# Unread matmuls of constants in TensorE's head: a gated linear attention recurrence followed by a squared-ReLU MLP

## The chip, the cores and the metric

The kernel runs on one core of a Trainium2 chip. The metric is the device time of one execution in microseconds (us), as the median of several runs. Before the change three runs took 197.0, 198.0 and 198.47 us, so the median is 198.0 us. One further execution was taken with the hardware profiler: it took 196.32 us, of which its profile covers a span of 194.6 us.

## The reference

For each of 4 batches and 8 heads a 48 x 48 state is decayed row by row, gets an outer product added, and is read by a query, for 768 steps. The 8 x 48 = 384 outputs of each of the 3072 tokens then go through a two-layer MLP of width 2048 with a squared ReLU.

```python
def _attn_ref(q, k, v, alpha):
    for t in range(S):                       # S = 768, D = 48
        state = alpha[:, :, t, :, None] * state + np.einsum('bhd,bhe->bhde', k[:, :, t], v[:, :, t])
        y[:, :, t] = np.einsum('bhd,bhde->bhe', q[:, :, t], state)
    return y

def _moe_ref(x, w_in, w_out):                # x: (3072, 384), w_in: (384, 2048), w_out: (2048, 384)
    h = x @ w_in
    r = np.maximum(h, 0.0)
    g = r * r
    return g @ w_out
```

## The kernel before, in words

**Tiling.** The tokens are cut into 24 chunks of 128 (6 for each batch). Within a chunk the recurrence is done as matrix products. For chunk g, in the order of its steps:

- Four loads on SP's queue (L384): alpha, k, q and v into one of 8 raw buffers, 192 KB each.
- `decay`: ACT takes the logarithm of alpha (`lab`, L394); TensorE makes running sums over the chunk with the triangular constant `LTRI` (L400, L402, into `psG`); ACT takes three exponentials (`asb` L406 and L408, `acs` L411); DVE scales k and q (`qks`, L417); GpSimd casts v (`vbf`, L421).
- `turned`: TensorE transposes the scaled k and q against the constant `IDENT` (8 matmuls, L432), and DVE copies them out (`qkt`, L435).
- `scores`: TensorE, 8 matmuls (L447); DVE masks the two results (`pm`, L453).
- `carry`: TensorE makes the chunk's contribution to the state (L467), DVE adds it (`ust`, L474), GpSimd decays it into the next state (`sbf`, L484).
- `mixed`: TensorE, state and scores times their right sides (L496, L500); ACT copies out (`xbf`, L507).
- `placed`: TensorE transposes the chunk's result (3 matmuls, L517), ACT writes it to `xt` (L521).
- `up`: four units for each chunk, each of 12 matmuls of 128 columns (L537) into one of two buffers `psH`; ACT applies the ReLU (`rr`, L542), DVE squares (`gt`, L544). Unit u of any chunk reads quarter u of the first weight matrix, `win`.
- `down`: four parts for each chunk, each of 4 matmuls of 384 columns (L553), accumulated in one of two buffers `psO`; after the fourth, ACT copies out (`osb`, L559) and SP stores (L561). Part p reads quarter p of the second weight matrix, `wout`.

**Order.** Nothing is ordered by hand. Every step is entered with its engine, an estimated duration and a due time (`add`); `order()` simulates the engines and the two load queues and fixes one order of instructions for each engine; `plan()` then places the waits on semaphores between engines. On the chip each engine runs its own list strictly in that order: an instruction that waits holds back everything behind it on its engine.

**The loads of the head.** The weights come in quarters on GpSimd's queue, tied to SP's loads: `weights` gates the first quarter of each group on the landing of a chunk's alpha, and `loads` gates the alpha load of chunks 3, 4 and 5 on the landing of a weight quarter. So the head contains this chain: GpSimd casts v of chunk 1, issues `win` quarters 0 and 1 (L365); when quarter 0 lands, SP issues alpha of chunk 3; when that lands, GpSimd issues `win` 2 and 3 and `wout` 0 and 1 (L369); when `wout` 0 lands, SP issues alpha of chunk 4; when that lands, GpSimd issues `wout` 2 and 3; when `wout` 2 lands, SP issues alpha of chunk 5. SP issues its loads in order.

**TensorE's order in the head**, the same in both kernels as far as the real work goes: sums 0, transposes 0, sums 1, scores 0, carry 0, transposes 1, mixed 0, placed 0, scores 1, sums 2, carry 1, mixed 1, transposes 2, placed 1, up unit 0 of chunk 0, scores 2, carry 2, up unit 1 of chunk 0, mixed 2, sums 3, placed 2, transposes 3, carry 3, scores 3, up unit 2 of chunk 0, mixed 3, then five up units without a break (the first of chunk 1, the last of chunk 0 and three more of chunk 1), and then the first down part. The kernel's two constants are written by GpSimd at the start (L338 to L343).

Of the kernel before, what the change touches and what calls it, by code (L numbers as in the profile page):

```python
# [32 lines left out]
class Program:  # L33
# [18 lines left out]
    def add(self, eng, fn, work, at, reads=(), writes=(), dma=None, nbytes=0, fast=False, behind=None):  # L52
        op = Op(len(self.ops), eng, fn, work, at, dma, nbytes, fast)
        for r in reads:
            for w in self.writer.get(r, ()):
                op.deps[w.n] = "raw"
        for r in writes:
            for w in self.writer.get(r, ()):
                op.deps.setdefault(w.n, "waw")
            for w in self.readers.get(r, ()):  # L60
                op.deps.setdefault(w.n, "war")
        for r in reads:
            if r not in writes:
                self.readers.setdefault(r, []).append(op)
        for r in writes:
            self.writer[r] = [op]
            self.readers[r] = []
        if dma is not None:
            last = self.slots.get(dma)
            if last is not None:  # L70
                op.deps.setdefault(last.n, "war")
            self.slots[dma] = op
        op.deps.pop(op.n, None)
        if behind is not None:
            op.deps.setdefault(behind.n, "order")
        self.ops.append(op)
        return op

    def order(self):
# [16 lines left out]
        def done(op, t, users):  # L96
            for u in users:
                known[u.n] = max(known[u.n], t)
                missing[u.n] -= 1
                if not missing[u.n]:  # L100
                    release(u, known[u.n])
# [42 lines left out]
        while left:  # L144
            best = None
            for e in ENGINES:
# [5 lines left out]
                while w and w[0][0] <= free[e]:  # L152
                    _, at, n = heapq.heappop(w)
# [13 lines left out]
            while w and w[0][0] <= t:  # L167
                _, at, n = heapq.heappop(w)
                heapq.heappush(r, (at, n))
            _, n = heapq.heappop(r)  # L170
            op = self.ops[n]
# [10 lines left out]
            else:  # L182
                same = [u for u in op.users if u.eng == e]
                done(op, free[e], same)
                done(op, free[e] + self.LATENCY[e], [u for u in op.users if u.eng != e])
        self.programs = programs

    def plan(self):
        place = {}
# [65 lines left out]
def bass_gla_recurrent__then__act_relu_squared_kernel(  # L255
# [21 lines left out]
    FT = DFF // 128  # L277
# [9 lines left out]
    NXB, NGT, NRR, NOS, NU, NAC = 2, 5, 4, 4, 2, 3  # L287

    def sb(name, shape, dt, n=None):
        if n is None:  # L290
            return nc.alloc_sbuf_tensor(name, shape, dt)
        return [nc.alloc_sbuf_tensor(f"{name}{i}", shape, dt) for i in range(n)]
# [13 lines left out]
    LTRI = sb("ltri", [128, 128], BF16)  # L306
    IDENT = sb("ident", [128, 128], BF16)
# [7 lines left out]
    psO = [nc.alloc_psum_tensor(f"psO{i}", [128, 512], FP32) for i in range(2)]  # L315
    psG = [nc.alloc_psum_tensor(f"psG{i}", [128, 512], FP32) for i in range(4)]

    pr = Program(nc)
    add = pr.add
# [33 lines left out]
    WH = 4  # L353
# [174 lines left out]
    def up(b, u, at):  # L528
# [4 lines left out]
        def mm(pe):  # L533
# [10 lines left out]
        add("DVE", lambda dve: dve.tensor_tensor(GT[b % NGT][:, FU * u:FU * u + FU, :], RR[r][:], RR[r][:], ALU.mult),  # L544
            430, at, reads=[("rr", r)], writes=[("gt", b % NGT, f) for f in range(FU * u, FU * u + FU)])

    def down(b, tt, p, at):
        n = CPB * b + tt
        ps, key, o = psO[n % 2], ("psO", n % 2), n % NOS

        def mm(pe):
            for fj in range(4 * p, 4 * p + 4):
                last = pe.matmul(ps[:, 0:DM], GT[b % NGT][:, fj, tt * 128:(tt + 1) * 128], WOUT[:, fj, :],  # L553
                                 start=(fj == 0), stop=(fj == FT - 1))
            return last
        add("PE", mm, 650, at, reads=[("gt", b % NGT, f) for f in range(4 * p, 4 * p + 4)] + [("wout", 4 * p * WH // FT)],
            writes=[key])
        if p == 3:
            add("ACT", lambda act: act.activation(OSB[o][:], ps[:, 0:DM], AF.Copy), 490, at,  # L559
                reads=[key], writes=[key, ("osb", o)])  # L560
            add("SP", lambda sp: sp.dma_start(out[n * C:(n + 1) * C, :], OSB[o][:]), 600, at,  # L561
                reads=[("osb", o)], dma=f"osb{o}", nbytes=C * DM * 4, fast=True)
# [8 lines left out]
    for b in range(NB):  # L571
        base = CPB * b + CPB + LAG
        for u in range(NU_):
            stages.append((base + u * CPB / NU_, lambda at, b=b, u=u: up(b, u, at)))
        for i in range(4 * CPB):
            stages.append((base + CPB + CPB / NU_ / 2 + i * CPB / (4 * CPB),
                           lambda at, b=b, i=i: down(b, i // 4, i % 4, at)))
    for at, fn in sorted(stages, key=lambda s: s[0]):
        fn(at)

    pr.order()
    pr.plan()

    with nc.Block() as block:
# [49 lines left out]
```

## Time and profile before

| what | value |
|---|---|
| median of three runs (lowest, highest) | 198.0 us (197.0, 198.47) |
| the profiled execution, and its span | 196.32 us, 194.6 us |
| TensorE matmuls busy in the span | 179.1 us (92%), 2464 instructions |
| ACT, DVE, GpSimd busy | 125.9 us, 118.7 us, 39.2 us |
| share of the chain that ended last on TensorE | 83% |
| the same for transfers (DMA) | 10% |
| TensorE busy from 50 to 160 us | 109.99 of 110 us |
| up matmuls (L537) | 1152, 222 ns each in the mean, 81.1 us |
| down matmuls (L553) | 384, 326 ns each in the mean, 76.6 us |
| weight quarters `win`, issue to landing | 5.5 to 7.0 us |
| weight quarters `wout`, issue to landing | 6.2 to 9.2 us |

How to read it. A busy time of a matmul runs from its start to its modelled end, and matmuls overlap, so the start of the next instruction says more of the pace than the duration of one. "Granted clock" is TensorE's clock as a share of full speed, recorded by the profiler. The chain that ended last is followed back from the last instruction, at each step to what released it. Durations and starts below are from that one execution, in us from the start of its span.

### The profile page before, as it was taken

Reading aid. Unit: us, or ns where it says so; the run is one execution under the profiler, and the core shown is the slowest. Engines: PE = TensorE matmul, PEld = TensorE weight load, DVE = VectorE, ACT = ScalarE, POOL = GpSimd, SP = SyncE. Lnnn points to the kernel's source line nnn. Section 1 sums busy time; section 2 is a strip of 40 time slices with the busy share of each in tenths; the row PEclk is TensorE's granted clock in tenths of the full one; section 3 lists DMA queues with packets and bytes.
Section 4 is the critical chain, followed back from the end, with each engine's and each line's share of the span. In section 5 each row is a group of like instructions: output and inputs, shape, how many; then the busy total and the mean of one; then the engine's idle time right before and its main releaser. Section 6 shows DMA issues by size and latency. Waiting matters only on the chain.

```text
span 194.6 us, 5761 instructions
## 1 busy us (share of the span) xinstructions
PE 179.1 (92%) x2464; PEld 143.5 (74%) x2464; DVE 118.7 (61%) x223; ACT 125.9 (65%) x261; POOL 39.2 (20%) x72
## 2 busy tenths in 40 slices
PE   1568589999999999999999999999999999999994
PEld 0346378787788878878877887888878887887772
DVE  4475754483657775775776775676677577585230
ACT  3534626747777766875786786786686687565751
POOL 2162541421111133133100302312110320220000
PEclk9999859999999999999999999999999999999999
DMA  6999899999989999898989979991110110111012
GB/s 124 204 188 163 159 173 203 142 167 189 207 174 190 187 187 228 180 221 166 226 190 214 221 158 211 193 215 70 45 40 3 40 44 0 44 44 40 3 40 81
DMA packets 107033, 27.11 MB, mean 139 GB/s; under 512 B 100352, under 2 KB 107008, under 8 KB 107008
## 3 DMA queue, kind: packets, MB, share of 16 engines
q1 hardware_dynamic: 103296, 23.60, 56.5%
q0 software_dynamic: 3712, 3.15, 11.3%
q8 instruction: 19, 0.31, 0.7%
q14 instruction: 6, 0.05, 0.1%
HBM read 25.17 MB, written 4.72 MB: 154 GB/s over the span
## 4 chain that ended last, share of the span: by engine, by line
PE 83%; DMA 10%; SPq 3%; ACT 1%; issue 1%; POOL 0%
PE psH L537 33%; PE psO L553 32%; DMA win<-in_moe_w_in_dram 6%; PE psG L432 5%; PE psG L447 3%; SPq L384 3%; PE psG L400 3%; DMA raw<-in_v_dram 2%; DMA raw<-in_alpha_dram 2%; PE psG L500 2%; PE psG L517 2%; PE psG L496 2%; PE psG L467 1%; PE psG L402 1%; ACT rr L542 1%
## 5 line engine op out<-in xcount | busy, mean ns | idle before, releaser
L537 PE MATMUL psH<-xt,win 128*128 128x128 bf16 x1152 | 81.1, 222 | 0.4
L542 ACT ACTIVATE rr<-psH 128x512 bf16<-128x512 f32 x96 | 57.1, 597 | 35.5 <-PE psH L537 34.8
L553 PE MATMUL psO<-wout,gt 128*128 128x384 bf16 x384 | 76.6, 326 | 0.0
L537 PEld LDWEIGHTS psH<-xt,win 128*128 128x128 bf16 x1152 | 69.1, 99 | 3.0 <-ACT rr L542 1.1
L544 DVE TENSOR_TENSOR gt<-rr 128x512 bf16<-128x512 bf16 x96 | 40.8, 426 | 39.9 <-ACT rr L542 39.9
L453 DVE TENSOR_TENSOR pm<-psG,ltri 128x512 bf16<-128x512 f32 x48 | 32.7, 688 | 17.7 <-PE psG L447 17.7
L553 PEld LDWEIGHTS psO<-wout,gt 128*128 128x128 bf16 x384 | 33.1, 97 | 13.8
L421 POOL CAST vbf<-raw 128x384 bf16<-128x384 f32 x24 | 14.1, 589 | 97.3 <-PE psG L500 49.4
L417 DVE TENSOR_TENSOR qks<-raw,asb 128x768 bf16<-128x768 f32 x24 | 22.8, 951 | 6.5 <-ACT asb L408 6.4
L484 POOL TENSOR_TENSOR sbf<-ust,acs 64x192 bf16<-64x192 f32 x32 | 17.5, 548 | 28.4 <-DVE ust L474 25.8
L435 DVE COPY qkt<-psG 128x1024 bf16<-128x1024 bf16 x24 | 16.6, 692 | 5.4 <-PE psG L432 4.8
L432 PE MATMUL psG<-ident,qks 128*128 128x128 bf16 x192 | 16.3, 234 | 3.7 <-DVE qks L417 3.7
L432 PEld LDWEIGHTS psG<-ident,qks 128*128 128x128 bf16 x192 | 13.6, 105 | 6.6 <-DVE qks L417 4.3
L394 ACT ACTIVATE lab<-raw 128x384 bf16<-128x384 f32 x24 | 12.5, 520 | 8.0 <-DMA raw<-in_alpha_dram 8.0
L521 ACT ACTIVATE xt<-psG 128x384 bf16<-128x384 bf16 x24 | 11.8, 491 | 6.6 <-PE psG L517 6.5
L559 ACT ACTIVATE osb<-psO 128x384 f32<-128x384 f32 x24 | 11.7, 488 | 6.2 <-PE psO L553 2.8
L406 ACT ACTIVATE asb<-psG 128x384 bf16<-128x384 f32 x24 | 11.8, 490 | 4.6 <-PE psG L402 3.4
L507 ACT ACTIVATE xbf<-psG 128x384 bf16<-128x384 f32 x24 | 11.8, 490 | 3.2 <-PE psG L500 3.1
L400 PE MATMUL psG<-lab,ltri 128*128 128x384 bf16 x24 | 8.5, 356 | 4.3 <-ACT lab L394 4.3
L408 ACT ACTIVATE asb<-psG 128x384 bf16<-128x384 f32 x24 | 11.8, 491 | 0.8
L500 PE MATMUL psG<-vbf,pm 128*128 128x48 bf16 x192 | 12.0, 189 | 0.0
L500 PEld LDWEIGHTS psG<-vbf,pm 128*128 128x128 bf16 x192 | 10.4, 100 | 1.5 <-DVE pm L453 0.3
(28 smaller groups left out, 102.6 us busy)
## 6 DMA issues: line engine op xcount, KB each, us to landing
raw<-in_alpha_dram SPq DMA_DIRECT2D x24, 192.0 KB, 3.9
raw<-in_k_dram SPq DMA_DIRECT2D x24, 192.0 KB, 4.1
raw<-in_q_dram SPq DMA_DIRECT2D x24, 192.0 KB, 4.2
raw<-in_v_dram SPq DMA_DIRECT2D x24, 192.0 KB, 3.8
out_dram<-osb SPq DMA_DIRECT2D x24, 192.0 KB, 3.1
win<-in_moe_w_in_dram POOLq DMA_DIRECT2D x4, 384.0 KB, 6.2
wout<-in_moe_w_out_dram POOLq DMA_DIRECT2D x4, 384.0 KB, 7.7
```

Of the source, the lines that this page charges most:

```text
L400: pe.matmul(ps[:, 0:HD], LTRI[:], LAB[l][:, :, 0:D])
L417: return dve.tensor_tensor(QKS[x][:, :, :, 0:D], in0, in1, ALU.mult)
L421: add("POOL", lambda e: e.tensor_copy(VBF[vb][:], RAW[r][:, 2, :]), 550, at, reads=[("raw", r, 2)], writes=[("vbf", vb)])
L432: last = pe.matmul(pt[:, j, :], flat[:, j * 128:(j + 1) * 128], IDENT[:], is_transpose=True)
L435: add("DVE", lambda dve: dve.tensor_copy(QKT[t][:].rearrange("p h s -> p (h s)"), ps[:].bitcast(BF16)), 700, at, reads=[key], writes=[key, ...
L453: add("DVE", lambda dve, i=i, ps=ps: dve.tensor_tensor(PMB[m][:, i, :, :], ps[:].rearrange("p (j s) -> p j s", j=NP), mask, ALU.mult), 690 ...
L484: add("POOL", lambda e, p0=p0, e0=e0, ac=ac: e.tensor_tensor(SBF[new][p0:p0 + 64, :, e0:e0 + D], UST[u][p0:p0 + 64, :, e0:e0 + D], ac, ALU ...
L500: last = pe.matmul(ps[:, h * D:(h + 1) * D], PMB[m][:, i, j, :], VBF[vb][:, h * D:(h + 1) * D], start=first, stop=(first or i == 1))
L537: last = pe.matmul(ps[:, f, :], WIN[:, kt, fj * 128:(fj + 1) * 128], XT[:, kt, b * TB:(b + 1) * TB], start=(kt == 0), stop=(kt == KT - 1))
L542: add("ACT", lambda act: act.activation(RR[r][:], ps[:], AF.Relu), 600, at, reads=[key], writes=[key, ("rr", r)])
L544: add("DVE", lambda dve: dve.tensor_tensor(GT[b % NGT][:, FU * u:FU * u + FU, :], RR[r][:], RR[r][:], ALU.mult), 430, at, reads=[("rr", r) ...
L553: last = pe.matmul(ps[:, 0:DM], GT[b % NGT][:, fj, tt * 128:(tt + 1) * 128], WOUT[:, fj, :], start=(fj == 0), stop=(fj == FT - 1))
```

## The change

`fill` is a new method of the planner. After `order()` has fixed the order, it goes through TensorE's list up to the first down part. Wherever the planner's own timetable leaves TensorE idle before an operation, it inserts as many matmuls as fit into 0.75 of that gap at 217 ns each. The inserted matmuls multiply `IDENT` by `LTRI` repeated four times (512 columns) into the two `psO` buffers. Nothing reads the result: the first matmul of a down part overwrites it. Besides these, one group of six such matmuls is entered as a step with an early due time; it waits for GpSimd's two constants.

The built kernel has 47 inserted matmuls, in 13 groups: 7 before sums 0, 7 before transposes 0, 2 before sums 1, 6 before transposes 1, 2 before placed 0, 4 before mixed 1, 2 before transposes 2, 2 before up unit 0, 4 before up unit 1, 6 before placed 2, 2 before carry 3, 2 before up unit 2, and 1 after mixed 3. The order of all other instructions on the five engines, and their waits, are as before, but for TensorE's wait for GpSimd's constants, which has moved from sums 0 and transposes 0 to the first inserted matmul.

```diff
+    def fill(self, fn, each, share, until):
+        out = []
+        end = None
+        for op in self.programs["PE"]:
+            if op is until:
+                until = None
+            if until is not None and end is not None and (op.start - end) * share > each:
+                n = int((op.start - end) * share / each)
+                idle = Op(len(self.ops), "PE", lambda pe, n=n: fn(pe, n), n * each, 0.0)
+                idle.start = end
+                self.ops.append(idle)
+                out.append(idle)
+            out.append(op)
+            end = op.start + op.work
+        self.programs["PE"] = out
...
+    downs = []
+
+    def busy(pe, n):
+        for i in range(n):
+            last = pe.matmul(psO[i % 2][:], IDENT[:], bass.AP(tensor=LTRI, offset=0, ap=[[128, 128], [0, 4], [1, 128]]))
+        return last
+
+    add("PE", lambda pe: busy(pe, 6), 2000, -6, reads=["ident", "ltri"], writes=[("psO", 0), ("psO", 1)])
+
...
-        add("PE", mm, 650, at, reads=[("gt", b % NGT, f) for f in range(4 * p, 4 * p + 4)] + [("wout", 4 * p * WH // FT)],
-            writes=[key])
+        op = add("PE", mm, 650, at, reads=[("gt", b % NGT, f) for f in range(4 * p, 4 * p + 4)] + [("wout", 4 * p * WH // FT)],
+                 writes=[key])
+        downs.append(op)
...
     pr.order()
+    first = next(o for o in pr.programs["PE"] if o in downs)
+    pr.fill(busy, 217, 0.75, first)
     pr.plan()
```

## The prediction

> **What bounds the kernel now.** I read the granted clock by stretches first, then the chain of waits, then the order of instructions around each load. From 50 us on TensorE is busy without a gap, and its last matmuls (20 of L553, start 188.27) end with the kernel but for one copy and a store. So the change can only move the moment from which TensorE no longer waits. The question is which moment that is.
>
> The clock, in windows of the head. Columns: window, its length, busy time of the five engines (instructions), granted clock, DMA share, GB/s.
>
> ```profile
> 22.50:23.00 0.50, 0.00 (x0) 0.00 (x0) 0.13 (x1) 0.47 (x2) 0.50 (x1) 1.00 0.69 138
> 23.00:23.50 0.50, 0.00 (x0) 0.00 (x0) 0.10 (x1) 0.47 (x3) 0.50 (x2) 0.80 0.91 108
> 23.50:24.00 0.50, 0.00 (x0) 0.00 (x0) 0.50 (x1) 0.46 (x2) 0.50 (x2) 0.50 0.71 104
> ...
> 30.00:30.50 0.50, 0.50 (x11) 0.50 (x9) 0.00 (x0) 0.04 (x1) 0.00 (x0) 0.87 1.31 200
> ```
>
> Between full and half speed, 0.80 puts the fall at 23.3 and 0.87 the rise at 30.13. The clock column also says 1.00 in every earlier window, but there the durations must be read: 12 up matmuls take 1.49 us at 17.78 and 0.83 us at 19.97. TensorE therefore ran at half speed up to about 19.9, fast to 23.3, at half speed to 30.13. The three turns lie 3.4 and 6.8 us apart, once and twice the same step.
>
> The chain of waits through the head. Columns: start, duration, what.
>
> ```profile
> 11.58 5.64 DMA win<-in_moe_w_in_dram
> ...
> 17.24 3.90 DMA raw<-in_alpha_dram
> ...
> 21.43 5.49 DMA win<-in_moe_w_in_dram
> ...
> 26.96 1.48 PE psH L537 x12
> ...
> 28.46 0.61 ACT rr L542
> ...
> 29.11 1.98 PE psH L537 x24
> ...
> 31.11 1.51 PE psH L537 x24
> ```
>
> Up to 26.92 loads set the time: each weight quarter opens an alpha load and that opens the next quarters. Only behind that does TensorE's half speed lie on the path, for some 3 us. But the load chain runs on beside it, which the order of instructions shows:
>
> ```profile
> 41.22 0.37 SPq L384 DMA_DIRECT2D raw<-in_alpha_dram  x1
> ...
> 44.24 1.46 PE L553 MATMUL psO<-wout,gt 128*128 128x384 bf16 x8
> ...
> 44.88 0.52 ACT L394 ACTIVATE lab<-raw 128x384 bf16<-128x384 f32 x1 [0.21 <-DMA raw<-in_alpha_dram]
> ...
> 45.54 0.33 PE L400 MATMUL psG<-lab,ltri 128*128 128x384 bf16 x1
> ```
>
> The alpha load of chunk 5 is issued at 41.22 when `wout` 2 lands, ACT sits idle 0.21 us for it, the logarithm ends at 45.40, and the sums of chunk 5 start at 45.54. No engine's speed is in that chain.
>
> **The change part by part.**
>
> *One inserted matmul.* No row has 512 columns. By the pace of starts, 12 up matmuls take 1.27 us at half speed (26.96 to 28.23), 106 ns for 128 columns, and 0.67 us fast; four 384-column down matmuls take 0.65 us fast, 163 ns each. By columns I estimate 423 ns at half speed and 217 ns fast; the bounds are 163 ns (the 384-column row) and 423. Their weight load (98 ns fast, 151 ns slow for L537) runs beside them. 47 of them are 10.2 us fast, 19.9 us slow.
>
> *Before 17.2 us (30 of the 47: 7, 7, 2, 6, 2, 4, 2).* The constants are ready at 2.08 (L343). The first seven at half speed end at about 5.1, so sums 0 start 0.8 us late (4.27 before). TensorE is then busy without a gap, and by the step read above (grid points 2.8, 6.2, 9.7 if its phase were the same) it is fast from 6.2, at the latest a step later. Sums and transposes then take about half (L432: 1.04 slow, 0.61 fast), so the lateness is gone by mixed 0. It would be free anyway: `win` 0 lands at 17.22 whatever TensorE does, and the only way from TensorE into the load chain is GpSimd's `sbf` of chunk 1 (L484, 17.13 to 18.21), after which GpSimd idles 3.21 us for alpha of chunk 3. Cost 0; with the cover gone it would be 0.8 us.
>
> *From 17.2 to 26.92 (2, 4, 6, 2, 2, from up unit 0 on).* They fill the gaps 20.64 to 21.53, 22.3 to 24.01 (TensorE idle 1.69 for ACT's `xbf`) and 25.8 to 26.96. The clock does not fall at 23.3. Transposes 3 go from 1.03 to 0.61, so `qkt`, scores 3 and `pm` come some 0.5 us earlier. Up unit 2 cannot: `win` 2 lands at 26.92.
>
> *From 26.92 on.* Up unit 2 takes 0.83 instead of 1.48 to its result: the ReLU starts 0.65 earlier, at 27.81, and the first up of chunk 1 at 28.46 instead of 29.11. The single inserted matmul after mixed 3 (0.22) lies in that wait: mixed 3 needs `pm`, by then at about 27.6, and takes 0.4, so TensorE has 28.3 against 28.46. The next 24 up matmuls take 1.51 (row 31.11) instead of 1.98, `win` 3 (issued 22.2, 6.8 to landing) being there at 29.0. Sum: 0.65 + 0.47 = 1.12 us gained at 31.1.
>
> *Where it goes.* Next late: `wout` 0 landed at 31.1, against a first down part at 32.2 then: free. Alpha of chunk 4 (landed by 35.04, when GpSimd issues `wout` 2): its logarithm, 35.34 before, can go to 35.04, and holds the ReLU behind it, so the gain shrinks to about 0.9. `wout` 2 landed at 41.2, and the down parts that read it start at 41.89: at most 0.67 left. The sums of chunk 5: logarithm end 45.40 plus 0.06 (the first sums, 4.27, followed a logarithm that ended at 4.21) is 45.46, against 45.54: at most **0.08 us left**. Behind that all is TensorE's queue in the same order (qks 5 ends at 48.13, its transposes start 48.42; no nearer limit). So against the profiled execution: 194.6 - 0.08 + 1.72 us outside the span = 196.24, from 196.32.
>
> *The median.* It is 198.0, 1.68 above the profiled execution, and all three runs lie above it. One thing that the trace lets differ between executions is where the 3.4 us steps fall. Steady work starts at 26.24; the clock could rise after the first whole step behind that, from 29.6 (26.24 + 3.4) to 33.0. Each us later than 30.13 costs half: the old kernel ends between 0.08 earlier (the limit above) and 1.4 later than its profile, about 0.6 in the mean. The new one should not have this spread, its clock being up already. Gain on the median: 0.08 to 1.5, taken as 0.65. **198.0 - 0.65 = 197.35, rounded to 197.4 us.**
>
> [...]
>
> **The rivals.**
>
> *A. The load chain does not hold the gain.* If the sums of chunk 5 are not tied so closely in other executions (that alpha landing 1 us earlier would do; the raw loads issued from 40 to 60 us took 3.6 to 5.2 us to land), the 1.12 us pass, and with the 0.6 of the phase 1.7 in all: 196.3. For it: all three runs are longer than the profiled one, which is room for the gain. Against: the ACT idle of 0.21 ended by that very landing.
>
> *B. Slower: the gate does not count these matmuls.* They multiply a 0/1 matrix by a 0/1 matrix, and no row shows such. At 423 ns the last 11 alone take 4.65 us, against 1.69 + 0.47 us and the 0.7 before `win` 2 that were idle: counted along the queue from 22.3 (6 x 0.423, placed 2, transposes 3, 2 x 0.423, carry, scores, 2 x 0.423), up unit 2 starts at 28.55 and the first up of chunk 1 at 30.9 instead of 29.11: 1.8 late. The clock then misses the step at 30.13 and rises at 33.5: another 0.8. 199.8 to 200.6. It decides once the lateness passes the 1.12 us won, and is over 1% from 2.0 us. Against it: the transposes, also against `IDENT`, were among the work that brought the clock up at 19.9.
>
> *C. It does nothing to the end.* The clock stays up, but the old kernel's median is long for another reason (loads, or time outside the span): 197.9.
>
> **How the numbers follow.** The forecast 0.52, A 0.24, B 0.10, C 0.14. One per cent is about what a measurement of this kernel can tell from no change: faster means under 196.0, slower over 200.0. Faster takes half of A and a tail of the forecast (the runs scatter by 0.5 to 1.0 about their median): 0.12 + 0.06 = 0.18. Slower is most of B: 0.08. Within: 0.74. The range reaches from the near end of A, 196.1, to C with the scatter of the runs (198.47), 198.5; that leaves out half of A and B.
>
> **What would show it.** Right: up matmuls fast from the first (12 in 0.83 at 17.3), granted clock 1.00 without a fall up to 50 us, up unit 2 still at 26.96, the first up of chunk 1 near 28.5, and then new idle time on TensorE before the down parts at 41 and before the sums of chunk 5, which stay at 45.4 to 45.5. A shows itself by sums 5 starting over 0.3 us earlier than 45.46, B by inserted matmuls at 400 ns and more after 10 us and a clock under 1.00 there. I am wrong if the loads themselves (landing of `win` 2, `wout` 2, alpha 5) move, or if the end moves by over 1 us while sums 5 stand still.

## The result and the profile after

The changed kernel takes 196.49 us in the median of 22 runs (195.19 to 197.89), the kernel before 198.0 us beside it (22 runs). The ratio is 0.9927, with a 95% interval of 0.9908 to 0.9947: 1.45 us faster, between 1.05 and 1.8. The prediction had 197.4 us and a gain of 0.65.

The profiled execution of the changed kernel took 196.7 us with a span of 195.0, longer than the profiled execution of before (196.32, 194.6). The two profiles alone would say that nothing was gained. Why they mislead is the main thing that this case teaches.

The page of the changed kernel, its clock and the row of the inserted matmuls (busy time and mean ns of one, idle time before them and its cause):

```profile
PEclk9999999999999999999999999999999999999999
...
L569 PE MATMUL psO<-ltri,ident 128*128 128x512 bf16 x47 | 14.3, 430 | 2.1 <-POOL ident L361 2.1
```

The same four windows as in the prediction:

```profile
22.50:23.00 0.50, 0.50 (x4) 0.20 (x2) 0.00 (x0) 0.47 (x2) 0.50 (x2) 1.00 0.90 169
23.00:23.50 0.50, 0.33 (x2) 0.00 (x0) 0.40 (x1) 0.47 (x3) 0.50 (x1) 1.00 0.84 108
23.50:24.00 0.50, 0.29 (x3) 0.17 (x3) 0.50 (x1) 0.15 (x1) 0.50 (x2) 1.00 1.22 173
30.00:30.50 0.50, 0.50 (x12) 0.45 (x9) 0.00 (x0) 0.50 (x1) 0.00 (x0) 1.00 1.31 200
```

The clock no longer falls at 23.3. The mean of 430 ns for an inserted matmul is the time to its modelled end; by their starts they follow each other every 423 ns at half speed (7 from 2.14 to 5.10) and every 215 to 216 ns fast (13 from 24.73 to 27.53 in experiment 7).

The order of instructions in the changed kernel, TensorE's and one line of ACT's:

```profile
27.58 0.84 PE L555 MATMUL psH<-xt,win 128*128 128x128 bf16 x12 [1.12 <-DMA win<-in_moe_w_in_dram]
28.64 0.38 PE L569 MATMUL psO<-ltri,ident 128*128 128x512 bf16 x1
29.11 3.91 PE L555 MATMUL psH<-xt,win 128*128 128x128 bf16 x60
...
41.86 1.48 PE L580 MATMUL psO<-wout,gt 128*128 128x384 bf16 x8 [0.37 <-DMA wout<-in_moe_w_out_dram]
...
44.77 0.52 ACT L412 ACTIVATE lab<-raw 128x384 bf16<-128x384 f32 x1
...
45.51 0.33 PE L418 MATMUL psG<-lab,ltri 128*128 128x384 bf16 x1
```

From the start of up unit 2 (27.58) to the first up of chunk 1 (29.11) it takes 1.53 us, 2.15 before. But up unit 2 waited 1.12 us for its weights, which landed 0.6 us later than in the profile of before, and then the down parts waited 0.37 us for `wout` 2. So the sums of chunk 5 (45.51) stand where they stood. The chain of waits names loads for most of this head:

```profile
11.47 5.42 DMA win<-in_moe_w_in_dram
...
16.90 4.07 DMA raw<-in_alpha_dram
...
22.84 8.56 DMA wout<-in_moe_w_out_dram
...
31.41 3.20 DMA raw<-in_alpha_dram
...
34.90 6.91 DMA wout<-in_moe_w_out_dram
```

Behind that the loads of this execution were slow again: TensorE lost 0.39 us more at 59.1, traced back by the chain to an alpha load (53.71, 3.68 us). Two executions with different luck in their loads cannot show a gain of 1 us.

### The profile page after: what moved, and what is told of

It reads as the page before. It is cut to its first block, busy times and chain, and to the rows that moved or that the text cites. A ratio compares the mean times of both kernels' runs of the same rounds, so it can differ in the third digit from the quotient of the medians.

```text
span 195.0 us, 5853 instructions
## 1 busy us (share of the span) xinstructions
PE 185.5 (95%) x2511; PEld 142.7 (73%) x2511; DVE 120.3 (62%) x223; ACT 125.6 (64%) x261; POOL 39.7 (20%) x72
## 4 chain that ended last, share of the span: by engine, by line
PE 68%; DMA 18%; SPq 9%; issue 1%; ACT 1%; POOL 1%; DVE 0%
PE psO L580 27%; PE psH L555 26%; SPq L402 9%; DMA wout<-in_moe_w_out_dram 8%; DMA raw<-in_alpha_dram 8%; PE psG L450 4%; PE psG L465 3%; DMA win<-in_moe_w_in_dram 3%; PE psG L418 2%; PE psG L518 2%; PE psG L535 2%; PE psG L514 1%; PE psG L485 1%; POOL win L383 1%; PE psG L420 1%
## 5 line engine op out<-in xcount | busy, mean ns | idle before, releaser
L555 PE MATMUL psH<-xt,win 128*128 128x128 bf16 x1152 | 79.4, 219 | 2.2 <-DMA win<-in_moe_w_in_dram 1.9
L555 PEld LDWEIGHTS psH<-xt,win 128*128 128x128 bf16 x1152 | 67.6, 98 | 5.8 <-DMA win<-in_moe_w_in_dram 2.9
L562 DVE TENSOR_TENSOR gt<-rr 128x512 bf16<-128x512 bf16 x96 | 41.7, 436 | 41.0 <-ACT rr L560 40.9
L439 POOL CAST vbf<-raw 128x384 bf16<-128x384 f32 x24 | 15.0, 624 | 98.3 <-PE psG L518 55.3
L435 DVE TENSOR_TENSOR qks<-raw,asb 128x768 bf16<-128x768 f32 x24 | 23.5, 979 | 7.2 <-ACT asb L426 7.1
L569 PE MATMUL psO<-ltri,ident 128*128 128x512 bf16 x47 | 14.3, 430 | 2.1 <-POOL ident L361 2.1
L450 PEld LDWEIGHTS psG<-ident,qks 128*128 128x128 bf16 x192 | 12.3, 98 | 4.6 <-DVE qks L435 2.2
L450 PE MATMUL psG<-ident,qks 128*128 128x128 bf16 x192 | 14.7, 219 | 0.6 <-DVE qks L435 0.4
L518 PE MATMUL psG<-vbf,pm 128*128 128x48 bf16 x192 | 11.3, 183 | 0.4 <-DVE pm L471 0.4
L518 PEld LDWEIGHTS psG<-vbf,pm 128*128 128x128 bf16 x192 | 9.6, 96 | 2.2 <-DVE pm L471 0.9
```

Source lines behind the costliest of these rows:

```text
L435: return dve.tensor_tensor(QKS[x][:, :, :, 0:D], in0, in1, ALU.mult)
L439: add("POOL", lambda e: e.tensor_copy(VBF[vb][:], RAW[r][:, 2, :]), 550, at, reads=[("raw", r, 2)], writes=[("vbf", vb)])
L450: last = pe.matmul(pt[:, j, :], flat[:, j * 128:(j + 1) * 128], IDENT[:], is_transpose=True)
L518: last = pe.matmul(ps[:, h * D:(h + 1) * D], PMB[m][:, i, j, :], VBF[vb][:, h * D:(h + 1) * D], start=first, stop=(first or i == 1))
L555: last = pe.matmul(ps[:, f, :], WIN[:, kt, fj * 128:(fj + 1) * 128], XT[:, kt, b * TB:(b + 1) * TB], start=(kt == 0), stop=(kt == KT - 1))
```

## The experiments

Each ratio is to the kernel before on the same chip, with its 95% interval. I write S for the start of up unit 2, which needs `win` 2, and "stretch" for the time from S to the start of the sums of chunk 5. From there to the last 20 down matmuls it takes 142.42 to 142.44 us in all profiles below (142.73 and 143.16 in the two shown first), and some 6.3 us more to the end, so S and the stretch decide the span. In the edits, `ups` lists the up units as `downs` does the down parts, and `places` the `placed` steps; the lines that fill these lists, and those that give `fill` one more argument, are left out.

Four theories of the gain were tried. Theory 1: the clock's rise falls at another moment in each execution of the kernel before, and the change takes away the late ones. Theory 2: the head's 1.1 us pass the load chain, the clock being much the same each time. Theory 3: the early chunks being sooner done is what pays. Theory 4, formed after experiments 1 to 4: the inserted matmuls shorten the stretch by 1.0 to 1.1 us, and the load chain decides from one execution to the next how much of it is kept.

**1. The kernel before once more** (no edit).

> The kernel before, unchanged, to see what its executions differ in: each lists its span and its mean granted clock. Theory 1 (the clock's rise falls at another moment in each execution, and the profiled one was early): mean clocks spread by at least 0.005 (in the profile, 0.981 goes with a rise at 30.13 us; each us later costs 0.5 us, so 0.01 less in the mean clock goes with up to 2 us more span), lower clocks have the longer spans, median near 198.0 us. Theory 2 (the gain of the change is the head's 1.1 us passing the load chain, the clock being much the same each time): clocks within 0.002 of 0.981, spans unrelated to them.

Measured: 197.08 us, ratio 0.9985 (0.9958 to 1.0012). Its 12 runs and the 68 runs of the kernel before that stand beside the two sets of timed experiments fall into three groups by mean clock (one further run, of 199.27 us at 0.974, is left out of the ratios and of these groups):

```
mean clock     runs   median us   lowest to highest
0.974          11     198.25      197.60 to 198.80
0.980-0.983    65     197.23      195.92 to 198.37
0.990-0.991     4     196.60      195.84 to 197.35
```

Lower clocks have the longer times, as theory 1 says, but most runs have the same clock as the profiled one (0.981) and still scatter by 2.4 us. Neither theory 1 nor theory 2 is enough. The clock comes in steps of about 0.0085: one period of 3.4 us more at half speed is 1.7 us in some 195, or 0.0087. (The last thousandths come from the end: in the first profile the clock falls once more at 194.0, behind all matmuls.) Weighted by the groups, the late rise costs 0.1 us in the mean (11 x 1.0 - 4 x 0.6, over 80), not 0.6.

**2. Only the early 30, and 3. only the late 17 matmuls.**

```diff
-    first = next(o for o in pr.programs["PE"] if o in downs)
+    first = next(o for o in pr.programs["PE"] if o in ups)
```

> Only the 30 inserted matmuls before the first up unit's group; none from up unit 0 on. Theory 1: the clock is up from about 6 us but falls again in the gaps of 20 to 24 us and rises at about 30 to 33 us as before, so the ratio to the kernel before is 0.998 to 1.002. Theory 2: the same. A third theory, that the early chunks being sooner done is what pays: 0.993 to 0.996.

```diff
-    add("PE", lambda pe: busy(pe, 6), 2000, -6, reads=["ident", "ltri"], writes=[("psO", 0), ("psO", 1)])
...
-    pr.fill(busy, 217, 0.75, first)
+    pr.fill(busy, 217, 0.75, next(o for o in pr.programs["PE"] if o in ups), first)
```

> Only the 17 inserted matmuls from the group before up unit 0 on. TensorE is slow up to about 18 to 20 us, then stays fast. Theories 1 and 2: the whole gain, ratio 0.991 to 0.995, mean clock close to 1.00 from 20 us on. Third theory (the early chunks): 0.998 to 1.002.

Measured: early alone 0.9992 (0.9963 to 1.0020), clocks 0.965 to 0.983; late alone 0.9946 (0.9925 to 0.9966), clock 1.0 in all 12 runs. Most of the gain, if not all, is in the 17 from up unit 0 on, and the third theory falls. The late version alone also scatters least: a standard deviation of 0.27 us against 0.70 of the unchanged kernel. Its order of instructions suggests why:

```profile
27.79 0.60 PE L573 MATMUL psO<-ltri,ident 128*128 128x512 bf16 x2
28.23 0.83 PE L558 MATMUL psH<-xt,win 128*128 128x128 bf16 x12
...
45.79 0.33 PE L420 MATMUL psG<-lab,ltri 128*128 128x384 bf16 x1
```

Up unit 2 follows the inserted matmuls without a wait. TensorE is at half speed to about 21.7 (the four inserted matmuls from 21.02 take 1.23 us, between 0.86 fast and 1.69 slow), and the first inserted groups delay it, so S here is TensorE's own 28.23 and not a landing.

**4. The changed kernel without the wait of chunk 5's alpha load.**

```diff
     pr.order()
+    load5 = alphas[5]
+    for d in [d for d in load5.deps if pr.ops[d].dma == "wout2"]:
+        del load5.deps[d]
```

> The changed kernel, with SP's alpha load of chunk 5 no longer waiting for the second weight matrix's quarter 2 to land (the only wait taken away; order as before). If the sums of chunk 5 at about 45.5 us are the floor that holds the changed kernel: ratio to the kernel before below the changed kernel's 0.9927, by 0.2 to 0.5 us (0.990 to 0.992), quarter 2 then landing later than 41.8 us and being the next limit. If the floor does not bind in most executions: 0.9927 within 0.002, or worse, since the loads share the transfer engines.

Measured: 0.9946 (0.9916 to 0.9977), not better than the changed kernel. The packets of the two load queues together took 105% of the time of the 16 transfer engines from 30 to 42 us in the kernel before (71.7 and 33.5%), so they do overlap there; but `wout` 2, issued at 34.77, released TensorE at 41.19 here, after 6.4 us, against 6.9 from issue to landing in the changed kernel. The order of instructions:

```profile
41.19 1.47 PE L583 MATMUL psO<-wout,gt 128*128 128x384 bf16 x8 [0.51 <-DMA wout<-in_moe_w_out_dram]
...
43.95 1.47 PE L583 MATMUL psO<-wout,gt 128*128 128x384 bf16 x8 [0.26 <-DMA wout<-in_moe_w_out_dram]
...
45.26 0.33 PE L421 MATMUL psG<-lab,ltri 128*128 128x384 bf16 x1
```

The logarithm of chunk 5 (start 43.86) now ends 0.89 us before the sums, and two waits for `wout` quarters, 0.77 us of idle time, stand in front of them: one wait has taken the place of another, so the ratio alone does not tell what the first one cost. The rows of the changed kernel's three profiles do: its logarithm ends 0.22, 0.46 and 0.30 us before the sums, which never wait for it. My limit at the sums of chunk 5 held none of them.

**5. and 6. A longer load chain, without and with the inserted matmuls.** The edit is that of experiment 4, and then, in both:

```diff
+    quarter3 = next(o for o in pr.ops if o.dma == "wout3")
+    load5.deps[quarter3.n] = "raw"
```

> The kernel before, with SP's alpha load of chunk 5 waiting for quarter 3 of the second weight matrix instead of quarter 2: the load chain is made longer by the time between their landings (2.0 us in the first profile, 41.2 and 43.2), all else as it was. In the five profiles so far the logarithm of that alpha ended 0.1 to 0.9 us before the sums of chunk 5 started. If the sums of chunk 5 can be held by the load chain: ratio to the kernel before 1.004 to 1.010 (1 to 2 us).

> The changed kernel with the same longer load chain. Theory 4 (the inserted matmuls shorten the stretch from the landing of win quarter 2 to the sums of chunk 5 by 1.0 to 1.1 us, and the load chain decides how much of that is kept): now both kernels are held at the same place, so the ratio of this kernel to the one with the longer chain and no inserted matmuls is 0.998 to 1.001, and the sums of chunk 5 wait for the logarithm. If the gain does not depend on the load chain, that ratio stays at 0.992 to 0.995.

Measured: 1.0046 (1.0012 to 1.0080) without, 1.0020 (0.9991 to 1.0050) with. The means of 12 runs each are 198.09 and 197.66 us, 0.43 apart with a standard error of 0.28. So less is left than the 1.45 of the change, as theory 4 says, but nothing left and most of 1 us left are both within that error. The profile with the matmuls shows the mechanism that I had predicted for the changed kernel, here made to happen (its clock fell too, in a wait of 1.68 us for `win` 2 before up unit 2; S is 27.89 and the stretch 19.70):

```profile
44.14 0.37 SPq L402 DMA_DIRECT2D raw<-in_alpha_dram  x1
...
47.02 0.52 ACT L415 ACTIVATE lab<-raw 128x384 bf16<-128x384 f32 x1 [1.20 <-DMA raw<-in_alpha_dram]
47.59 0.34 PE L421 MATMUL psG<-lab,ltri 128*128 128x384 bf16 x1 [0.74 <-ACT lab L415]
```

**7. Twice the late matmuls** (41 in place of 17).

```diff
-    pr.fill(busy, 217, 0.75, next(o for o in pr.programs["PE"] if o in ups), first)
+    pr.fill(busy, 217, 1.5, next(o for o in pr.programs["PE"] if o in ups), first)
```

> 41 inserted matmuls from the group before up unit 0 on, in place of 17 (twice the share of the gaps). Clock up as with 17. At 216 ns the 13 before placed 2 take 2.8 us against a gap of 1.7, and the following groups another 3 us: up unit 2 starts 0.5 to 1.5 us later than the landing of its weights, and 2 more matmuls lie directly before the first up of chunk 1. Expected 1.0 to 2.0 us more than with 17: ratio to the kernel before 0.999 to 1.005. If the inserted matmuls cost nothing wherever they stand (weights are the limit to 27 us): 0.993 to 0.996 again.

Measured: 1.0071 (1.0042 to 1.0101), 2.5 us more than with 17. TensorE's order:

```profile
24.73 2.97 PE L573 MATMUL psO<-ltri,ident 128*128 128x512 bf16 x13
...
30.04 1.25 PE L573 MATMUL psO<-ltri,ident 128*128 128x512 bf16 x5
31.13 0.83 PE L558 MATMUL psH<-xt,win 128*128 128x128 bf16 x12
```

S is 31.13 with no wait before it: 2.9 us later than with 17. The stretch, 17.68 (31.13 to 48.81), is that of a fast clock. TensorE is busy without a gap from 18.3 to 31.9, so there an inserted matmul takes its time from the real work; of the 24 more (5.2 us at 216 ns) about half is paid, and the rest fills idle time.

**8. Only the six matmuls in the longest gap.**

```diff
-            if until is not None and end is not None and (op.start - end) * share > each:
+            if op is only and (op.start - end) * share > each:
...
-    add("PE", lambda pe: busy(pe, 6), 2000, -6, reads=["ident", "ltri"], writes=[("psO", 0), ("psO", 1)])
...
-    pr.fill(busy, 217, 0.75, first)
+    pr.fill(busy, 217, 0.75, places[2])
```

> Only 6 inserted matmuls, before placed 2, in the longest gap of the kernel before (1.69 us from 22.3). If the fall of the clock hangs on that gap alone, it stays up until the up matmuls run without a break: mean clock 0.998 to 1.0 and ratio 0.993 to 0.996. If the shorter gaps (0.9 us at 20.6, 1.1 us at 25.8) are enough to bring it down in the next step: clocks of 0.98 to 0.99 and 0.996 to 1.001.

Measured: 1.0000 (0.9964 to 1.0035), clocks from 0.983 to 1.0. The gap at 22.3 was filled, but in the profile the clock fell one step later, in a wait for `win` 2. Two rows of the order of instructions, then windows (columns as in the prediction):

```profile
22.25 1.46 PE L569 MATMUL psO<-ltri,ident 128*128 128x512 bf16 x6
...
28.33 1.46 PE L555 MATMUL psH<-xt,win 128*128 128x128 bf16 x12 [2.04 <-DMA win<-in_moe_w_in_dram]
```

```profile
27.00:27.50 0.50, 0.00 (x0) 0.00 (x0) 0.50 (x2) 0.00 (x0) 0.00 (x0) 0.89 1.15 178
...
34.00:34.50 0.50, 0.50 (x10) 0.50 (x9) 0.31 (x1) 0.04 (x1) 0.00 (x0) 0.79 1.18 235
```

Mixed 3 stood behind that wait in TensorE's list: its last input, the masked scores, was written by 27.62, and it started at 29.58. The clock rose only at 34.2, and the stretch was 19.68 us: the late rise that theory 1 speaks of exists, and here it cost 1.1 us against the 18.5 to 18.6 of the kernel before. The 12 runs differ in this: in four the clock stayed up (0.999 to 1.0) and the median is 196.4 us, in the eight others (0.983 to 0.991) it is 197.5.

**9. to 12. Two more profiles of each kernel** (no edits).

> The kernel before, unchanged, one more profile. Theory 4: from the start of up unit 2 (win quarter 2) to the sums of chunk 5 it takes 18.6 to 18.8 us with a clock that rises at most 3.5 us after that start, and up to 1 us more with a later rise; TensorE does not wait for a load in between. If the loads paced the head in this kernel too, the stretch would contain such a wait.

> The same again: 18.6 to 18.8 us, more only with a clock rise later than 3.5 us after the start of up unit 2.

> The changed kernel, one more profile. Theory 4: clock up throughout; from the start of up unit 2 to the sums of chunk 5 17.56 us, plus what TensorE waits in between for wout quarters 2 and 3 or for the logarithm of chunk 5 (0 to 0.8 us in the profiles so far).

> The same again: 17.56 us plus the waits for wout quarters 2 and 3 and for the logarithm of chunk 5.

Measured: 197.89 and 197.85 us for the kernel before, 196.07 and 194.45 for the changed one (one run each). The order of instructions in the first of these profiles of the kernel before (the third in the table below):

```profile
28.91 1.46 PE L539 MATMUL psH<-xt,win 128*128 128x128 bf16 x12 [1.43 <-DMA win<-in_moe_w_in_dram]
31.05 4.29 PE L539 MATMUL psH<-xt,win 128*128 128x128 bf16 x60
...
46.42 0.52 ACT L396 ACTIVATE lab<-raw 128x384 bf16<-128x384 f32 x1
...
47.40 0.33 PE L402 MATMUL psG<-lab,ltri 128*128 128x384 bf16 x1
```

and in the second of the changed kernel (the third in the table):

```profile
26.49 0.84 PE L558 MATMUL psH<-xt,win 128*128 128x128 bf16 x12
28.02 3.92 PE L558 MATMUL psH<-xt,win 128*128 128x128 bf16 x60
...
43.99 0.33 PE L421 MATMUL psG<-lab,ltri 128*128 128x384 bf16 x1
```

The profiles of the kernel before, of the changed one and of experiments 2 to 5, read off the same rows:

```
profile                            S      stretch   TensorE's waits for loads in it   span
before, shown first                26.96  18.58     0                                 194.6
before, once more                  28.80  18.62     0                                 196.1
before, third                      28.91  18.49     0                                 196.1
before, fourth                     28.88  18.51     0                                 196.1
changed, shown first               27.58  17.93     0.37 (wout 2)                     195.0
changed, second                    28.12  17.49     0                                 194.3
changed, third                     26.49  17.50     0                                 192.7
late 17 only                       28.23  17.56     0                                 194.5
early 30 only                      27.33  18.74     0                                 194.8
before, load 5 behind wout 3       28.44  18.73     0                                 195.9
changed, load 5 without its wait   26.76  18.50     0.77 (wout 2 and 3)               194.0
```

The stretch is 18.5 to 18.6 in the kernel before, 18.7 in two variants whose clock falls as well, and 17.5 to 17.6 with the late matmuls once the waits are taken off. (In the row of experiment 4 it takes the starts to see that: its two waits, 0.77 us of idle time, put the down parts off by 0.59 and 0.41 us, and 18.50 - 1.00 is 17.50.) Theory 4 holds, with a gain of 1.02 us (18.51 to 17.49). And in three of four executions of the kernel before `win` 2 lands 1.9 us later than in the one on which I built the prediction.

## Why the prediction was right, and where it was wrong

- **An inserted matmul**, 217 ns fast and 423 ns slow: measured 216 and 423.
- **The early 30 cost nothing**: right. Sums 0 start at 5.10 (I had 5.1), up unit 0 at 17.47, and the early part alone changes the time by 0.1%.
- **The clock stays up from 17 to 27 us**, transposes 3 in 0.62: right. So is that up unit 2 cannot gain, which waits for `win` 2.
- **From up unit 2 on**: right in mechanism and size. 0.62 of the 0.65 us to the first up of chunk 1 came; the sum of 1.12 us is 1.02 by the stretch.
- **"At most 0.08 us left"** is a step that failed. It was true of one execution. There `win` 2 landed at 26.92, early against the rest of the load chain, so TensorE was early too and reached the sums of chunk 5 just behind the logarithm. In the third profile of before S is 28.91 while `wout` 2 lands at 41.88, only 0.7 later than in the first; its down parts start 1.9 us behind that landing, so there 1.02 us would pass. In the changed kernel's profiles the sums of chunk 5 start at 45.51, 45.61 and 43.99, and what waits there is for `win` 2 and `wout` 2 (0.37 us once), not for that logarithm. Experiment 4 shows that taking the wait away buys nothing, experiments 5 and 6 that a longer chain can hold part of the gain. The prediction's own sign of being wrong, loads that move, is what came: S lies between 26.49 and 28.91.
- **The median.** I put its 1.68 us above the profiled execution on the clock's phase, 0.6 in the mean. The clock accounts for 0.1. Its phase does differ (it falls at 23.3, 25.2, 25.1 and 25.1 in the four profiles), but it rose 3.0 to 3.3 us after S in all of them, so the stretch stayed the same. The rest goes with the landing of `win` 2: S is 1.9 us later in the three other profiles, and their spans are 1.5 longer. Four profiles do not prove that this is the whole of it.
- **The sum.** 1.02 of the stretch and 0.1 of the clock make 1.1 us, against 1.45 with an interval of 1.05 to 1.8; I had 0.65. The late matmuls alone won 1.07 (0.67 to 1.48). The right size came from the term that I had worked out as 1.12 and then cut to 0.08; in its place I had put a mean of 0.6 for the clock's phase, which is worth 0.1. That two errors of opposite sign left 197.4 within 1 us of the result is luck. Whether something more is gained, S being earlier in some profiles with the early matmuls (26.49 to 28.12, and 27.33 with the early part alone) than in the other three of before, is not settled: transfers of the same quarter scatter by 1.5 us (5.49 to 6.99 for `win` 2 in the kernel before), and the early part alone gives 0.9992.
- **Rival A** was nearest: the gain passes the load chain. Its condition (alpha of chunk 5 landing 1 us earlier) came in one profile, where that load was there by 43.16, when its logarithm started, against 44.88; in the kernel before it was mostly `win` 2 that landed later. **Rival B** is refuted by the 216 ns and the clock of 1.00; experiment 7 shows its other half, that matmuls beyond the gaps are paid for. **Rival C** is refuted by the ratio.
- **Where the clock fell**: at 23.3 (before), 0.98 us into the gap between the two rows below (22.32 to 24.01), and at 27.4 (experiment 8), 1.10 us into a wait of 2.04. It stayed up through waits of 1.12 and 1.28 us (changed, first and second profile).

```profile
22.08 0.24 PE L402 MATMUL psG<-ltri,lab 128*128 128x1 bf16 x4
24.01 0.50 PE L517 MATMUL psG<-ident,xbf 128*128 128x128 bf16 x3 [1.69 <-ACT xbf L507]
```

The half-speed stretches of the profiles last 6.8 us, 10.2 (early 30 only) and 3.4 (experiment 6): two, three and one times 3.4 us wherever S lies, with mean clocks of 0.981 to 0.983, 0.974 and 0.991.

## What to carry to other kernels

A slack of a tenth of a microsecond against a load, read from one execution, is no limit (0.08 us here, with S between 26.96 and 28.91 in four profiles): ask first how far that load's landing scatters, and take the gain of the engine's own stretch as the forecast until several profiles show the wait. Here the clock fell in waits of 1.69 and 2.04 us, and filling the gaps with unread matmuls paid as long as they fit: 17 gave a ratio of 0.9946 with the clock at 1.0 in all 12 runs, the same matmuls doubled and more (41) cost 2.5 us, and with one group alone the clock was at 0.983 to 0.991 in eight of 12 runs. Compare two profiles by stretches between fixed points (from a landing to a step) and not by their spans when the difference is near 1 us.

## What the runs showed of the hardware that was not expected

- The same transfer in the same program, `win` 2 of 384 KB in GpSimd's queue, took 5.5 to 7.0 us from issue to landing in the four profiles of the kernel before (5.49, 6.88, 6.64, 6.99; issued at 21.43 to 22.22). By its place in the load chain this moved the whole kernel: S from 26.96 to 28.80, 28.91 and 28.88, the span from 194.6 to 196.1.
- The mean granted clocks of 80 executions of the kernel before lie in three groups (0.974, 0.980 to 0.983, 0.990 to 0.991), those of 22 executions of the changed one at 0.998 to 1.0. The profiles show half speed for 6.8 us in the four of the kernel before (0.981 and 0.982) and for 3.4 us in experiment 6 (0.991).
- In these 14 profiles the falls are better told by the busy share of 3.4 us than by the length of one gap. In the 3.4 us up to its fall TensorE was busy 1.69 us (before, 19.9 to 23.3), 1.54 us (experiment 6, 24.5 to 27.9) and 1.70 us (experiment 8, 24.0 to 27.4), and 1.33 to 1.66 us in the five other profiles in which the clock fell: half and less. In the six in which it stayed up, no stretch of 3.4 us between 18 and 35 us held less than 2.09 us (changed, 24.2 to 27.6).
- At half speed, 3.4 us with 2.22 us busy (before, 23.3 to 26.7) and with 2.42 us (experiment 8, 27.4 to 30.8) left the clock down, both more than those 2.09. After the fall the first 3.0 to 3.3 us from S on ran at half speed too, in all four profiles of the kernel before.
- Behind matmuls of a 0/1 matrix with a 0/1 matrix, whose result nobody reads, TensorE ran at full speed: eight transposes took 0.62 us at 7.99 in the changed kernel, 1.04 at 6.95 before, and from 16 to 38 us the granted clock was 1.00 in every half microsecond of the changed kernel's three profiles, 0.50 from 23.3 to 30.13 in the first of before.
